# In the attention's tail: two e buffers of three PSUM banks, transposes in the sums' bank, dummies in the projections' bank

## The chip, the core and the metric

The kernel runs on one core of one Trainium2 chip. Its engines work side by side, each in the order of its own program: TensorE (PE) multiplies matrices and transposes, VectorE (DVE) and ScalarE (ACT) work elementwise and read PE's results, GpSimd (POOL) works elementwise on the main on-chip memory, SyncE (SP) issues most of the transfers. PE's results lie in PSUM, which this kernel treats as eight banks of 512 float32 columns for each of 128 partitions. An instruction that needs another engine's result, or a bank that another engine still reads, waits for it, and all that stands behind it on its engine waits too.

The metric is the device time of one execution in microseconds (us), the median of several runs.

## The reference

One transformer block on x of 2048 tokens by 640 features, in float32. The condition c gives six vectors (shift, scale and gate for each half). First half: a layer norm with shift and scale, attention with 32 heads of 20 features in which each token sees itself and the 255 tokens before it, the projection wo, a gate and a residual. Second half: a layer norm with shift and scale, then a channel MLP of width 1536 (which normalises once more), a gate and a residual.

```
scores = jnp.einsum("bhqd,bhkd->bhqk", q, k) * (Dh ** -0.5)
mask = (idx[:, None] - idx[None, :] >= 0) & (idx[:, None] - idx[None, :] < W)
scores = jnp.where(mask[None, None], scores, -1e9)
p = _softmax(scores, axis=-1)
o = jnp.einsum("bhqk,bhkd->bhqd", p, v)
...
x = x + ga * _A_ref(h, A_wqkv, A_wo)
h = _layernorm(x, axis=-1) * (1 + cb) + sb
x = x + gb * _B_ref(h, B_w1, B_b1, B_w2, B_b2)
```

## The kernel before

The attention goes over two halves of the tokens, eight quads of four heads in each, and eight blocks of 128 tokens in each quad: n = 128 items. A loop over t = 0 to 144 (line 1308) runs several stages of this at different lags, and everything that it issues keeps the program's order on each engine.

In iteration t, for t < 128, scores s of item t (queries by keys) are computed for their row maximum (`s_batch`, `s_max`). From LAG = 11 on, scores e of item t - 11 (keys by queries) follow (`e_batch`): four heads with up to 384 columns each. DVE masks e (`e_mask`), ACT takes the exponential into pt (`e_exp`), and POOL cuts two triangles out of pt. At two further iterations' lag the sums o = p v are formed (`pv_stage`, 24 small matmuls) and ACT copies them out to oT (`pv_copy`). The copy stands before `e_exp` in ACT's program, except in the iterations of SUMS_LAST (line 64), where it stands behind it; of 128 to 141 these are 129 to 133, 135, 136 and 139. An item whose mask isn't "do" (the first and the last key block of a quad in the second half: here the items of iterations 130, 131 and 138) has a longer mask and an exponential over 1536 columns instead of 1024.

Besides, a `plan` gives to each quarter h of an iteration other work: the projections before the attention, transposes, and from iteration 115 on the block's next stage for the first token blocks (`mid_steps`): the projection wo (`womm`, tiles in the projections' bank "pp"), the add of its result to x on DVE, layer norms, transposes of x (`xtrans`, tiles xt, copied by ACT to xT) and of y (`ytrans`, tiles yt, read by ACT for yhi and by DVE for ylo). `aside` gives a transpose its bank: "a" before iteration 11, then "o", the bank of the sums, and from iteration 128 on "t", a bank of its own. In iterations 128 to 141 the asides are: 128 the transpose of the row maxima (pm); 129 yt with three blocks; 130 yt with two; 131 xt with four; 132 xt with one; 134 yt; 135 yt; 137 xt with four; 138 xt with one; 140 yt with three; 141 yt with two.

WARM (line 74) puts dummy matmuls into some quarters; before iteration 128 they write the bank "pp", after that a bank of their own, "k". In the tail they stand in 129, 130, 135, 136 and 141.

From iteration 128 on no s is left. That stretch, to the first matmul of the MLP, is the tail; the last e is that of iteration 138, the last sums those of 141. `turn_scores` closes the pools of e and s there and opens e anew.

`width` (line 546) gives the columns between two heads in a score tile: 512 outside of iterations 11 to 127, so that a tile takes four banks and each head has one, and 384 within, so that it takes three and the heads lie across the banks' borders. `cuts` splits a head's product at the borders. The first two of the four slots use one half of the array's rows, the last two the other, and `score_batch` orders the pieces; where both halves write one bank, an empty PE instruction waits for the first half's piece before the second half's is issued.

PSUM in the tail: "pp" one bank from the left, "t" one next to it; "o" the first from the right, then four for e and one for "k". After the loop all pools but the left ones are closed; then `ps_h`, the MLP's first tile, is opened as first pool from the right, and `ps_out` behind it.

```
def aside(shape, name):
    kind = "a" if now[0] < LAG else "o" if now[0] < 2 * NQB * QUADS else "t"
    return pools[kind].tile(shape, F32, tag=kind, name=name)
...
def width():
    return 384 if LAG <= now[0] < 2 * NQB * QUADS else 512
```

Every instruction stands in the profile under line 116, the helper that keeps the order; so the groups are told apart by their tiles (e, s, o, pt, oT, xt, xT, yt, yhi, ylo, wo, warm).

Of the kernel before, what the change touches and what calls it, by code (L numbers as in the profile page):

```python
# [9 lines left out]
F32 = mybir.dt.float32  # L10
# [5 lines left out]
PSUM = bass.MemoryType.PSUM  # L16

P = 128
# [5 lines left out]
NQB = HALF // P  # L24
QUADS = H // 4
# [2 lines left out]
VQ = 4 * VW + 11  # L28
NSLOT = 3
NVB = 5  # L30
LAG = 11
PVLAG = 2
RUN0 = 33
# [40 lines left out]
WARM = {(115, 0): 2, (127, 2): 1, (129, 2): 4, (130, 1): 4, (135, 0): 7, (136, 0): 10, (141, 1): 1}  # L74
# [47 lines left out]
def block_kernel(ctx: ExitStack, tc: tile.TileContext, x, wqkv, wo, w1, b1, w2, b2, c, crow, wmod, wcol, sel, outT):  # L122
# [77 lines left out]
    sco_ctx = ExitStack()  # L200
    pools = {}
# [4 lines left out]
        for name, ctx_, side in (("p", ctx, "left"), ("o", att_ctx, "right"), ("s", sco_ctx, "right"), ("a", sco_ctx, "right")):  # L206
            open_banks(name, ctx_, side)

    def open_banks(name, ctx_, side="right"):
        pools[name] = ctx_.enter_context(  # L210
            tc.tile_pool(name=f"ps_{name}", bufs=1, space=PSUM, side=side, reuse_waits="tile")
        )

    def turn_scores(t, n):

        if t in (LAG, n):
            sco_ctx.close()
            for name in ("e", "s") if t == LAG else ("e",):
                open_banks(name, sco_ctx)

    def aside(shape, name):

        kind = "a" if now[0] < LAG else "o" if now[0] < 2 * NQB * QUADS else "t"
        return pools[kind].tile(shape, F32, tag=kind, name=name)


# [157 lines left out]
    kb_ = [att.tile([P, 2, 256 + HALF], F32R, name=f"kbuf{i}") for i in range(NSLOT)]  # L384
    vq_ = [att.tile([P, NQB, VQ], F32, name=f"vbuf{i}") for i in range(NVB)]
    vcar = att.tile([P, QUADS, 2, VQ], F32, name="vcar")
# [31 lines left out]
    def vblk(half, quad, kb):  # L418
        if half == 1 and kb < 0:
            return vcar[:, quad, kb + 2]  # L420
        return vq_[(half * QUADS + quad) % NVB][:, kb]

# [3 lines left out]
    now = [-1]  # L426
# [12 lines left out]
    def unit(half, kind, j, c2, eng, acc=None, late=False):  # L439
# [44 lines left out]
        def v_turn(b0, nb):  # L484
            def go():
# [13 lines left out]
                for h, d0, n, cnt, r0 in runs:  # L499
                    quad = h // 4  # L500
                    nq = half * QUADS + quad - NVB
                    assert nq < 0 or nq in done_v, (half, j, quad)
                    kb = 4 * c2 + b0
                    dst = vq_[(half * QUADS + quad) % NVB][:, kb : kb + nb]
                    c0 = (h % 4) * VW + d0
# [7 lines left out]
                    if half == 0 and kb + nb == NQB:  # L513

                        last_v[quad] = last_v.get(quad, 0) + cnt * DH + (0 if cnt else n)
                        if last_v[quad] == 4 * DH:
                            nc.gpsimd.tensor_copy(vcar[:, quad], vq_[quad % NVB][:, NQB - 2 : NQB])

# [25 lines left out]
        return t, t.rearrange("p (h n) -> p h n", n=n)[:, :, 0:384]  # L544

    def width():
        return 384 if LAG <= now[0] < 2 * NQB * QUADS else 512

    def cuts(slot, col, n):

# [100 lines left out]
    def e_batch(it):  # L651
        half, quad, i = it["key"]
        t, e = score_banks("e", f"e{half}_{quad}_{i}")
        parts = []
        for h in HEADS:
            pair, r = 2 * quad + h // 2, slice(64 * (h % 2), 64 * (h % 2) + 62)
            parts.append([(
                col, n, kbuf(half, pair)[r, 256 + kb * P : 256 + (kb + 1) * P],
                lambda off, n, q=qbuf(half, pair), r=r, q0=q0: q[r, q0 * P + off : q0 * P + off + n],
            ) for kb, q0, q1, col, n in e_parts(it)[0]])  # L660
        return (t, parts), e

    def e_mask(it, e):
        if it["mask"] == "do":

            nc.vector.copy_predicated(e[:, :, 0:P], masks["d"].to_broadcast([P, 4, P]), e[:, :, 2 * P : 384])
            return
        two = e.rearrange("p h (a n) -> p h a n", n=P)[:, :, 0:3:2]
        nc.vector.copy_predicated(
            two, masks[it["mask"]][:, None].to_broadcast([P, 4, 2, P]), negc[:, None].to_broadcast([P, 4, 2, P])  # L670
        )
# [310 lines left out]
    warm = ps_0.tile([P, P], F32, tag="w0", name="warm")  # L982
# [151 lines left out]
    def take_aside(t, go):  # L1134

        t += AFTER.get(taken[0], 0)
        taken[0] += 1
        while t in asides:
            t += 1
        asides.add(t)  # L1140
        put(t, 1, go)
        return t
# [38 lines left out]
    _, where, turns = lay_units(hi)  # L1181
# [34 lines left out]
    for half in range(2):  # L1216
# [4 lines left out]
        for quad in range(QUADS):  # L1221
            if half or quad:
                js = range(4 * quad * DH // P, (4 * quad * DH + 4 * DH - 1) // P + 1)
                due = 8 * (half * QUADS + quad)
                for c2 in range(2):
                    t = due + 4 * c2 - READ
                    for kind in range(2):
                        t = max([t, due - 8 * NSLOT + LAG + 8] + [over_at.get((kind, j, c2), -9) + 2 for j in js])
                        assert t < due + 4 * c2 - 1, (half, quad, c2, t)
                        put(max(t, 0), 3, lambda half=half, quad=quad, kind=kind, c2=c2: rows_in(half, quad, kind, c2))  # L1230
                        t += 1
    for n, ((g, at), lo) in enumerate(zip(((2, 0), (4, 1), (3, 2)), MODS)):
        steps, rows = mod_steps(g, at)
        spread(plan, [step(1, f) for f in steps], lo[0], lo[1])
        t = int(lo[1])
        for f in rows:
            t = take_aside(t, f) + 1
    for ch, when in turns.items():
# [7 lines left out]
        t = when  # L1246
        for kt in range(KT):
            t = take_aside(t, lambda gos=turn[3 * kt : 3 * kt + 3]: [go() for _, go in gos]) + 1
# [36 lines left out]
    for t, nm, go in sorted(tail, key=lambda e: e[:1]):  # L1285
        t = t if t < 128 else 128 + (t - 128) / LATE
        if nm not in ("load", "om"):
            t = max(t, TOMID)
# [12 lines left out]
    n = len(s_items)  # L1301

    pv_at = {}
    for half in range(2):
        for quad in range(QUADS):
            for qb in range(NQB):
                pv_at.setdefault(LAG + PVLAG + (half * QUADS + quad) * NQB + qb + half, []).append((half, quad, qb))
    for t in range(n + LAG + PVLAG + 4):
        now[0] = t
        si = s_items[t] if t < n else None  # L1310
        u = t - LAG
        ei = e_items[u] if 0 <= u < n else None
        turn_scores(t, n)
        if t == n:
            if WARM:
                pools["k"] = sco_ctx.enter_context(tc.tile_pool(name="ps_k", bufs=1, space=PSUM, side="right"))
            pools["t"] = ctx.enter_context(
                tc.tile_pool(name="ps_t", bufs=1, space=PSUM, side="left", reuse_waits="tile")
            )
        turn_m = 8 <= t <= n and t % 8 == 0  # L1320
        batches = []
        if ei and ei["kbs"]:
            batch, e = e_batch(ei)
            batches.append(batch)
        if si:
            batch, *got = s_batch(si)
            batches.append(batch)
        score_batch(batches)
        if ei and ei["kbs"]:
            e_mask(ei, e)  # L1330
        sums = [(*key, pv_stage(*key)) for key in pv_at.get(t, ())]
        if t not in SUMS_LAST:
            for each in sums:
                pv_copy(*each)
        if ei and ei["kbs"]:
            e_exp(ei, e)
        if t in SUMS_LAST:
            for each in sums:
                pv_copy(*each)
        if si:  # L1340
            s_max(si, *got)
        for h in range(4):
            if (t, h) in WARM:
                ps = pools["k"].tile([P, P], F32, tag="k", name=f"warm{t}_{h}") if t >= n else pools["p"].tile([P, P], F32, tag="pp", name=f"warm{t}_{h}")
                for _ in range(WARM[t, h]):
                    matmul(ps, idn, idn, start=True, stop=True)
            if h == 1:
                rows_out()
            if h == 1 and turn_m:
                m_rows(s_items[t - 1])  # L1350
            for go in plan.pop((t, h), ()):
                go()
        for key in pv_at.get(t, ()):
            pv_store(*key)
    assert not writes and not plan
    sco_ctx.close()
    att_ctx.close()


    mp = ctx.enter_context(tc.tile_pool(name="mp", bufs=1, side="right", reuse_waits="tile"))  # L1360
    ps_h = ctx.enter_context(tc.tile_pool(name="ps_h", bufs=1, space=PSUM, side="right", reuse_waits="tile"))
# [27 lines left out]
    for ch in range(nch):  # L1389
# [24 lines left out]
        for f in range(FT):  # L1414
# [7 lines left out]
            pool, tag = (ps_out, f"o{KT - 1}") if (ch, f) == (0, 1) else (ps_h, "h")  # L1422
# [70 lines left out]
```

## Time and profile before

| what | us |
|---|---|
| median of 3 runs | 977.62 (977.16 to 978.79) |
| the profiled execution, its own time | 978.3 |
| its span, first to last instruction | 976.6 |
| PE busy | 947.7 (97%) |
| DVE busy | 592.9 (61%) |
| POOL busy | 485.8 (50%) |
| ACT busy | 442.4 (45%) |
| weight loads on PE (beside the matmuls) | 752.6 (77%) |
| mean granted clock of TensorE | 0.998 |

A row of the timeline gives the start from the span's start, the duration, the engine, the operation, the tiles as out<-in, their shape, and how many instructions are merged in it; in square brackets stands how long the engine was idle ahead of it and what ended that. The operands in a matmul's name can stand in either order. A PE duration is that of a single pipelined instruction, so the distance between two starts says more. A row of the list of waits gives the waiting engine and tile, what it waited for, and the total, the number and the longest. A row of the table of stretches gives begin and end, length, busy time and number of instructions of PE, PEld (weight loads), DVE, ACT and POOL, the granted clock, and the DMA's share and rate.

### The profile page before, as it was taken

To read this page: it belongs to the slowest core of one execution; us is meant where nothing else is said; L and a number is where in the kernel's file an instruction comes from. 1 tells how busy PE (TensorE), PEld (TensorE's weight loads), DVE (VectorE), ACT (ScalarE), POOL (GpSimd) and SP (SyncE) were. 2 spreads that over 40 slices of the span, in tenths; PEclk is the share of its full clock that TensorE was granted. 3 is DMA by queue.
4 is the path that set the end of the run, shared out by engine and by line. 5 is a ranking of instruction groups with operands and counts; after the bars stand their busy time and mean duration, and the time that the engine had idled before them with its cause. 6 is when DMAs were issued, how large, how long until landed. Compare 5 with 4: busy or idle time off the path is not lost.

```text
span 976.6 us, 20093 instructions
## 1 busy us (share of the span) xinstructions
PE 947.7 (97%) x7789; PEld 752.6 (77%) x7789; DVE 592.9 (61%) x999; ACT 442.4 (45%) x777; POOL 485.8 (50%) x673
## 2 busy tenths in 40 slices
PE   8899999999999999999898999999999999999998
PEld 8677777777777777777677787888888888888886
DVE  6564977978776786767888556563534444342112
ACT  3724555666644545555545654434333243333222
POOL 4423555677864364553646844654554454332121
PEclk9999999999999999999999999999999999999999
DMA  8366778756778459854852245444423342114113
GB/s 307 99 207 199 243 226 260 224 170 168 220 231 236 121 174 283 241 155 120 224 161 76 81 137 161 127 130 138 138 57 103 115 144 85 54 57 145 54 43 119
DMA packets 98974, 152.17 MB, mean 156 GB/s; under 512 B 8864, under 2 KB 42112, under 8 KB 98880
## 3 DMA queue, kind: packets, MB, share of 16 engines
q1 hardware_dynamic: 89664, 142.50, 48.2%
q10 hardware_dynamic: 9216, 8.39, 2.7%
q8 instruction: 62, 1.02, 0.4%
q14 instruction: 32, 0.26, 0.1%
HBM read 98.51 MB, written 51.58 MB: 154 GB/s over the span
## 4 chain that ended last, share of the span: by engine, by line
PE 82%; DVE 7%; ACT 4%; POOL 2%; DMA 2%; issue 2%; SPq 1%; DVEq 0%; POOLq 0%; ACTq 0%
PE pp L116 17%; PE out L116 16%; PE h L116 16%; PE e L116 8%; PE o L116 7%; PE wo L116 7%; PE s L116 4%; ACT pt L116 3%; DVE e L116 2%; PE ppo L116 2%; DVE nm L116 1%; PE yt L116 1%; PE pv L116 1%; PE xt L116 1%; DMA wc<-in_wcol 1%
## 5 line engine op out<-in xcount | busy, mean ns | idle before, releaser
L116 POOL TENSOR_SCALAR_AFFINE_SELECT pt<-pt 128x512 f32<-128x512 f32 x192 | 127.7, 665 | 131.8 <-ACT pt L116 119.4
L116 ACT ACTIVATE pt<-e 128x1024 f32<-128x1024 f32 (+1 forms) x120 | 133.7, 1115 | 67.2 <-DVE e L116 63.8
L116 DVE TENSOR_REDUCE nm<-s 128x1 f32<-128x256 f32 (+5 forms) x212 | 158.0, 779 | 4.4
L116 POOL TENSOR_TENSOR w2lo<-w2r,w2hi 128x640 fp32r<-128x640 f32 x48 | 78.7, 1639 | 160.2 <-ACT w2hi L116 160.2
L116 DVE CAST ghi<-g 128x512 fp32r<-128x512 f32 x48 | 28.1, 585 | 155.7 <-ACT g L116 155.7
L116 PE MATMUL e<-qbuf,kbuf 62*128 62x128 f32 (+2 forms) x773 | 112.8, 330 | 9.1 <-ACT pt L116 7.6
L116 PEld LDWEIGHTS e<-qbuf,kbuf 62*128 62x128 f32 x773 | 81.2, 186 | 48.5 <-ACT pt L116 23.2
L116 PE MATMUL pp<-hhi,w_hi 128*128 128x512 f32 x265 | 113.4, 428 | 0.2 <-ACT pf L116 0.2
L116 PE MATMUL s<-kbuf,qbuf 60*128 60x384 f32 (+2 forms) x728 | 106.6, 303 | 4.0 <-DVE nm L116 1.6
L116 PE MATMUL pp<-hlo,w_hi 128*128 128x512 f32 x265 | 108.1, 408 | 1.3 <-POOL hlo L116 1.3
L116 DVE COPY_PREDICATED e<-mask_t,e 128x512 f32<-128x512 uint32 x96 | 66.6, 694 | 66.2 <-PE e L116 62.6
L116 PE MATMUL pp<-hhi,w_lo 128*128 128x512 f32 x265 | 106.8, 403 | 0.0
L116 PEld LDWEIGHTS s<-kbuf,qbuf 60*128 60x128 f32 x728 | 89.8, 187 | 14.0 <-DVE nm L116 6.1
L116 PE MATMUL o<-pt,vbuf 128*32 128x128 f32 x2688 | 99.6, 277 | 0.7 <-ACT xT L116 0.7
L116 PE MATMUL out<-ghi,w2hi 128*128 128x512 f32 x240 | 95.5, 398 | 0.5 <-ACT g L116 0.5
L116 PE MATMUL out<-glo,w2hi 128*128 128x512 f32 x240 | 94.0, 391 | 0.0
L116 PE MATMUL out<-ghi,w2lo 128*128 128x512 f32 x240 | 93.9, 391 | 0.0
L116 POOL TENSOR_TENSOR w_lo<-wraw,w_hi 128x128 fp32r<-128x128 f32 x171 | 76.0, 475 | 32.6 <-ACT w_hi L116 32.6
L116 PE MATMUL h<-yhi,w1hi 128*128 128x512 f32 x220 | 87.8, 399 | 0.0
L116 PE MATMUL h<-ylo,w1hi 128*128 128x512 f32 x220 | 86.2, 392 | 0.0
L116 PE MATMUL h<-yhi,w1lo 128*128 128x512 f32 x220 | 86.0, 391 | 0.0
L116 DVE COPY_PREDICATED s<-mask_t,s 128x512 f32<-128x512 uint32 x112 | 77.1, 689 | 11.8 <-PE s L116 11.5
(179 smaller groups left out, 1839.0 us busy)
## 6 DMA issues: line engine op xcount, KB each, us to landing
w2r<-in_w SPq DMA_DIRECT2D x48, 320.0 KB
qbuf<-q_scr SPq DMA_DIRECT2D x60, 240.0 KB
wraw<-in_wqkv SPq DMA_DIRECT2D x36, 320.0 KB
kbuf<-k_scr SPq DMA_DIRECT2D x44, 240.0 KB
q_scr<-stage SPq DMA_DIRECT2D x20, 512.0 KB
k_scr<-stage SPq DMA_DIRECT2D x20, 512.0 KB
o_scr<-oT ACTq DMA_DIRECT2D x64, 128.0 KB
wm<-in_wmod SPq DMA_DIRECT2D x20, 320.0 KB
```

The lines of the kernel that those rows point to most:

```text
L116: return self.tc.keep_in_program_order(op(*args, **kw))
```

## The change

From iteration 128 on e has a pool of two buffers, and the distance between heads stays 384, so that a buffer takes three banks: six in all, beside "pp" and "o". The banks "t" and "k" are not there: transposes use the sums' bank "o" to the end of the loop, and dummies the bank "pp". After the loop "t" is opened for the MLP.

```diff
+END = 1000
...
-    def open_banks(name, ctx_, side="right"):
+    def open_banks(name, ctx_, side="right", bufs=1):
         pools[name] = ctx_.enter_context(
-            tc.tile_pool(name=f"ps_{name}", bufs=1, space=PSUM, side=side, reuse_waits="tile")
+            tc.tile_pool(name=f"ps_{name}", bufs=bufs, space=PSUM, side=side, reuse_waits="tile")
         )
...
             for name in ("e", "s") if t == LAG else ("e",):
-                open_banks(name, sco_ctx)
+                open_banks(name, sco_ctx, bufs=1 if t == LAG else 2)
...
-        kind = "a" if now[0] < LAG else "o" if now[0] < 2 * NQB * QUADS else "t"
+        kind = "a" if now[0] < LAG else "o" if now[0] < END else "t"
...
     def width():
-        return 384 if LAG <= now[0] < 2 * NQB * QUADS else 512
+        return 384 if LAG <= now[0] else 512
...
         turn_scores(t, n)
-        if t == n:
-            if WARM:
-                pools["k"] = sco_ctx.enter_context(tc.tile_pool(name="ps_k", bufs=1, space=PSUM, side="right"))
-            pools["t"] = ctx.enter_context(
-                tc.tile_pool(name="ps_t", bufs=1, space=PSUM, side="left", reuse_waits="tile")
-            )
...
-                ps = pools["k"].tile([P, P], F32, tag="k", name=f"warm{t}_{h}") if t >= n else pools["p"].tile([P, P], F32, tag="pp", name=f"warm{t}_{h}")
+                ps = pools["p"].tile([P, P], F32, tag="pp", name=f"warm{t}_{h}")
...
     att_ctx.close()
-
+    now[0] = END
+    pools["t"] = ctx.enter_context(tc.tile_pool(name="ps_t", bufs=1, space=PSUM, side="left", reuse_waits="tile"))
```

## The prediction

> **What bounds the kernel now.** I read first where the span goes, then the stretch that the change touches, then its waits.
>
> ```profile
> span 976.6 us, 20093 instructions
> 538.08:578.07 39.99, 38.46 (x537) 30.64 (x537) 22.33 (x46) 24.56 (x43) 27.10 (x43) 1.00 0.27 80
> PEld e L116 <- ACT pt L116: 3.0, 6, 1.1
> PE e L116 <- ACT pt L116: 1.3, 2, 0.9
> ```
>
> The second line is the table of stretches (length, then busy time of PE, PEld, DVE, ACT, POOL, then clock) for the attention's tail, from the first scores of iteration 128 to the first matmul of the MLP. TensorE (PE) is busy 38.46 of 39.99 us there, at full clock, so the tail ends when PE has got through its program. PE executes in program order: each wait of one of its instructions delays everything behind it, and each microsecond added to the tail is added to the end, since what follows is matmuls again. The last two lines are the list of waits in the tail (total, times, longest): the scores e wait for the exponential (ACT, pt) of the tile before. That is what a second buffer can take away: 1.3 us as gaps between matmuls, at most 3.0 us as gaps between weight loads. I take 2.4, since some 0.1 us of each of the six load gaps is the normal step from one group to the next (an estimate).
>
> **The change part by part.** The tail's own order on PE, with every edited place in it:
>
> ```profile
> 538.08 0.62 PE L116 MATMUL e<-qbuf,kbuf 62*128 62x384 f32 x4
> 538.63 0.86 PE L116 MATMUL o<-pt,vbuf 128*32 128x128 f32 x24
> 539.42 0.28 PE L116 MATMUL pm<-idn,nm 128*32 128x128 f32 x1
> ...
> 541.01 0.62 PE L116 MATMUL e<-qbuf,kbuf 62*128 62x384 f32 x4 [0.42 <-ACT pt L116]
> ...
> 542.36 0.55 PE L116 MATMUL yt<-idn,y 128*128 128x128 f32 x3
> ...
> 543.73 0.68 PE L116 MATMUL e<-qbuf,kbuf 62*128 62x256 f32 x8
> ...
> 546.12 0.38 PE L116 MATMUL yt<-idn,y 128*128 128x128 f32 x2
> 547.36 0.73 PE L116 MATMUL e<-qbuf,kbuf 62*128 62x128 f32 x8 [0.86 <-ACT pt L116]
> ...
> 549.36 0.60 PE L116 MATMUL xt<-idn,xb 128*128 128x128 f32 x4
> ...
> 550.97 0.62 PE L116 MATMUL e<-qbuf,kbuf 62*128 62x384 f32 x4
> ...
> 552.86 0.27 PE L116 MATMUL xt<-idn,xb 128*128 128x128 f32 x1
> ...
> 556.37 0.62 PE L116 MATMUL e<-qbuf,kbuf 62*128 62x384 f32 x4
> ...
> 557.72 0.55 PE L116 MATMUL yt<-idn,y 128*128 128x128 f32 x3
> ```
>
> These are iterations 128 to 132 and 134. In each the transpose (pm, yt, xt) comes 1.34, 1.35, 2.39, 2.00, 1.89 and 1.35 us after its e. It writes a bank of its own, so it does not ask whether the sums o of the same iteration have been copied out.
>
> First, **e in three banks**. At 384 columns a head the four heads' products fall on bank borders: six pieces instead of four (nine instead of eight where a tile has two key blocks), and the middle bank is written by both halves of the array, so a wait for the first half's piece stands before the last. The trace has the same six pieces in the same order, alone, as scores s in the main loop:
>
> ```profile
> 153.62 0.89 PE L116 MATMUL s<-kbuf,qbuf 60*128 60x256 f32 x6
> 154.44 0.75 PE L116 MATMUL o<-pt,vbuf 128*32 128x128 f32 x20
> ```
>
> From the first piece to the next group 0.82 us pass; for four pieces (538.08 to 538.63) 0.55. So +0.27 us for each of eleven e tiles, 3.0 us. Below it could be 0 if the wait cost nothing; above, 0.54 a tile if the nine-piece tiles stop twice. I take 0.27, from the row of the same shape.
>
> Second, **transposes in the sums' bank**. A transpose must now wait for the copy oT of that iteration's sums, and the next sums for the copy of the transpose. The main loop, which already does this, shows both waits:
>
> ```profile
> 509.69 0.28 PE L116 MATMUL pm<-idn,nm 128*32 128x128 f32 x1 [1.11 <-ACT oT L116]
> 516.12 0.86 PE L116 MATMUL o<-pt,vbuf 128*32 128x128 f32 x24 [0.74 <-ACT xT L116]
> ```
>
> How long it takes is a chain through DVE and ACT, of which these are the steps:
>
> ```profile
> 539.56 0.27 ACT L116 COPY oT<-o 128x128 f32<-128x128 f32 x1 [1.54 <-PE o L116]
> 541.74 0.70 DVE L116 COPY_PREDICATED e<-mask_t,e 128x512 f32<-128x512 uint32 x1 [0.62 <-PE e L116]
> 542.48 1.02 ACT L116 ACTIVATE pt<-e 128x1024 f32<-128x1024 f32 x1 [0.21 <-DVE e L116]
> 543.39 0.26 ACT L116 COPY oT<-o 128x128 f32<-128x128 f32 x1
> ...
> 548.14 1.29 DVE L116 COPY_PREDICATED_SCALAR e<-mask_t,negc 128x1024 f32 x1
> 549.47 1.46 ACT L116 ACTIVATE pt<-e 128x1536 f32<-128x1536 f32 x1 [0.28 <-DVE e L116]
> 550.82 0.26 ACT L116 COPY oT<-o 128x128 f32<-128x128 f32 x1
> ```
>
> ACT runs in program order too. Where the iteration is not in SUMS_LAST the copy comes before the exponential: it starts 0.93 after o (538.63 to 539.56), takes 0.27, and ACT's end reaches PE 0.04 later (549.47 + 1.46 to 550.97); with e's 0.82 before it, the transpose can start 2.06 after e. Where the iteration is in SUMS_LAST the copy stands behind the exponential, and that behind the mask, and that behind e: 0.73 (541.01 to 541.74) + 0.27, then 0.74 to the exponential, 0.91 to the copy, 0.27 and 0.04, in all 2.96 after e. With the long mask and exponential of the tiles that have no causal pair: 0.78 + 0.27 + 1.33 + 1.35 + 0.26 + 0.04 = 4.03. By this:
>
> - 128 (not last): from 1.34 to 2.06, +0.72. Here pm is the maximum's transpose.
> - 129 (last): from 1.35 to 2.96, +1.61.
> - 130 and 131 (last, long): from 2.39 and 2.00 to 4.03, +1.64 and +2.03.
> - 132 (last): from 1.89 to 2.96, +1.07.
> - 134 (not last): from 1.35 to 2.06, +0.71.
> - 133, 135, 136 and 137: no new wait; in 133 there is no transpose, in 135 the seven dummies stand ahead of it, in 136 there is none, in 137 nine matmuls stand ahead. Only e's pieces, 4 x 0.27 = +1.08.
>
> Those are +8.86, e's pieces counted in. The tail's end has three more places:
>
> ```profile
> 569.66 0.53 PEld L116 LDWEIGHTS e<-qbuf,kbuf 62*128 62x128 f32 x8 [0.35 <-ACT pt L116]
> 572.25 0.86 PE L116 MATMUL o<-pt,vbuf 128*32 128x128 f32 x24
> ...
> 575.90 0.55 PE L116 MATMUL yt<-idn,y 128*128 128x128 f32 x3
> 576.82 0.86 PE L116 MATMUL o<-pt,vbuf 128*32 128x128 f32 x24
> 577.00 0.56 DVE L116 TENSOR_TENSOR ylo<-yt,yhi 128x384 fp32r<-128x384 f32 x1 [2.94 <-ACT yhi L116]
> 577.93 0.38 PE L116 MATMUL yt<-idn,y 128*128 128x128 f32 x2
> 578.07 0.49 PE L116 MATMUL h<-yhi,w_hi 128*128 128x512 f32 x1
> 578.76 0.42 DVE L116 TENSOR_TENSOR ylo<-yt,yhi 128x256 fp32r<-128x256 f32 x1 [0.81 <-ACT yhi L116]
> ```
>
> - 138: the transpose x1 is copied out behind the long exponential, 1.05 + 1.33 + 1.35 + 0.26 + 0.04 = 4.03 after e, and the sums of 139 now wait for it. Before they came 2.59 after e (569.66 to 572.25): +1.44.
> - 140: the sums of 141 wait until ylo has read yt: 575.90 to 577.56 is 1.66, and 0.04; before they came 0.92 after yt: +0.78.
> - 141: yt waits for the sums' copy, 0.93 + 0.27 + 0.04 = 1.24 after o. And the MLP's first tile h is laid in the bank that o leaves (both are the first pool opened from the right), so it waits for the last ylo: 578.76 + 0.42 - 577.93 = 1.25, and 0.04. So h comes 2.53 after o, before 1.25 (576.82 to 578.07): +1.28.
>
> Third, **dummies in the projections' bank**: they now wait for the add that reads it. In 129, 130, 135 and 136 the transposes or e keep PE later than that add anyhow; in 141 the wait for the copy covers it. Cost 0; uncovered it would be under the 0.49 of one add each (an estimate from ylo's rows of like size). Nothing moves past SP's or POOL's queues; what they carry in the tail shifts with it.
>
> The sum: 8.86 + 1.44 + 0.78 + 1.28 = 12.4, less the e waits, 2.4: +10.0 us. Note that in every iteration above the transpose starts after the copy that follows the exponential, or PE has work until then: the second buffer is hardly ever used ahead of time, and the wait for e has turned into a longer one for o. Behind the tail a little may come back, since PE waits once for ACT there and DMAs would be relatively earlier:
>
> ```profile
> 588.40 0.50 PE L116 MATMUL out<-ghi,w2hi 128*128 128x512 f32 x1 [0.52 <-ACT g L116]
> ```
>
> Between 0 and 0.52; I take 0.4. So +9.6. The profiled execution took 978.3 us (span 976.6), 0.7 over the median 977.62 of the runs shown; on the median that is 987.2.
>
> **The rivals.** A clock drop. In the main loop one gap was followed by a slower PE clock:
>
> ```profile
> 488.51 0.55 PE L116 MATMUL e<-qbuf,kbuf 62*128 62x128 f32 x5 [2.00 <-ACT pt L116]
> 490.00:492.00 2.00, 2.00 (x29) 1.78 (x20) 1.97 (x3) 1.26 (x2) 0.00 (x0) 0.60 0.00 0
> ```
>
> The gap was 2.00 us, and the granted clock (third column from the end) 0.60 in the next stretch: 0.8 us lost in 2 us. The tail now has no such gap and clock 1.00. The new waits come near it: in 131 the transpose starts 4.03 after e, of which e, o and one step of the projection fill about 2.2, so some 1.8 us are empty, with 1.3 to 1.4 empty in 129 and 130 just before (estimates from the rows above). One drop costs 0.8 to 1.6 us; at 1.2 the time is 988.4. The Trainium skill (TensorE: Matmul & The Clock Gate, Why this matters for your kernels) asks only that gaps between bursts of matmuls stay under about 3 us. By that rule no drop follows and 987.2 stands; the row above shows a drop after a gap of 2.00 us, so the trace does not agree, and I keep the drop as a case.
>
> The pieces of e cost nothing: if the wait in front of the last piece is covered, 11 x 0.27 = 3.0 fall away: 984.2. For it speaks that in the main loop two tiles' pieces are woven into each other; against it that in the tail e stands alone, as s does in the quoted row.
>
> The waits for e stay beside those for o, so that the second buffer does nothing at all: 987.2 + 2.4 = 989.6. Against it: by the walk above PE reaches the next e later than the exponential ends, so there is nothing left to wait for.
>
> The other side: the sums' copy is never late. The place is ACT's order in 129 to 132, the price the transposes' waits; if these and the pieces' cost vanish, the e waits are all that is left: 977.6 - 2.4 = 975.2. It decides at the copy's end against PE's arrival: in 129 PE has finished o 1.6 us after e, the copy ends 2.9 after it, so it would have to end 1.3 us sooner. For it speaks that ACT is busy only 24.56 of 39.99 us; against it that the copy's place behind the exponential is program order, and that the exponential's own start hangs on the mask. The Trainium skill (Perfetto Trace Analysis, Optimization Strategy) says that one gap recurring on the engine that should be full can mean too few buffers for the next tile. By that rule alone the recurring waits for e go and the time is this rival's; the trace agrees that the gaps recur (six of them) but not that they are large.
>
> **How the numbers follow.** The forecast, +9.6 to 987.2, has 0.52; a clock drop (988.4) 0.27; free pieces (984.2) 0.12; e waits that stay (989.6) 0.04; the other side 0.05, of which I give 0.03 to faster and 0.02 to a result where only half of it holds. Faster or slower means by over 0.2%, about 2 us, which is what a measurement of this kernel can tell from no change. All cases but the last lie above that: slower 0.95, same 0.02, faster 0.03. The range: down by free pieces (3.0) and e waits at their upper end (0.6) to 983.6; up by e waits at 1.3 instead of 2.4 (1.1), nothing given back behind the tail (0.4), the pieces' upper end (three times 0.27, 0.8) and one drop (1.2) to 990.7. The cases left out hold under 2 in 10.
>
> **What would show it right or wrong.** In the profile of the changed kernel the tail, from the first e without s to the first h, should last about 50 us instead of 40. PE's waits there should name ACT oT ahead of pm, yt and xt (1.3 to 1.9 us each in 129 to 131), ACT xT ahead of the sums of 139 (over 1 us) and DVE ylo ahead of the sums of 141 and of h; waits of e for ACT pt should be near 0. From the first piece of an e tile to o about 0.82 us. A granted clock under 1.00 in the tail would show the drop. I am wrong if transposes start within 0.2 us of the matmul ahead of them in 129 to 132, or if the tail is under 45 us.

## The result and the profile after

| | before | changed |
|---|---|---|
| median of four runs each, us | 977.39 (976.78 to 978.79) | 986.71 (986.50 to 989.09) |
| the profiled execution, us | 978.3 | 986.5 |
| its span, us | 976.6 | 984.8 |
| mean granted clock | 0.998 | 0.998 |

The changed kernel is slower: the ratio of the times is 1.0091, with a 95% interval from 1.0078 to 1.0104. On the medians it loses 9.3 us, between the two profiled executions 8.2.

The table of stretches of the changed kernel, for its tail and for all that follows it (length, busy time of PE, PEld, DVE, ACT and POOL, granted clock, DMA):

```profile
537.64:588.13 50.49, 42.42 (x557) 33.67 (x556) 23.24 (x48) 25.60 (x45) 26.68 (x43) 1.00 0.26 78
588.13:984.80 396.67, 392.52 (x1900) 330.37 (x1900) 165.26 (x297) 133.04 (x211) 167.18 (x170) 1.00 0.35 106
```

The stretch behind the tail in the kernel before, from the same view:

```profile
578.07:976.60 398.53, 393.10 (x1903) 330.32 (x1901) 166.07 (x298) 133.74 (x212) 167.44 (x170) 1.00 0.35 108
```

So the 8.2 us split into three: the tail went from 39.99 to 50.49 (+10.50), what follows it from 398.53 to 396.67 (-1.86), and what precedes it from 538.08 to 537.64 (-0.44, in code that the change doesn't touch: in the profile of before the clock falls to half there for 3.41 us from 490 on, in that of the changed kernel it doesn't, and the groups ahead of 490 differ by 0.02 us only). PE is busy only 42.42 of 50.49 us in the tail, where it was busy 38.46 of 39.99: it now waits. The list of PE's waits in the changed kernel's tail (total, times, longest) names for what:

```profile
PE yt L117 <- ACT oT L117: 2.8, 3, 1.3
PE xt L117 <- ACT oT L117: 2.0, 2, 1.4
PE o L117 <- ACT xT L117: 1.0, 1, 1.0
PE h L117 <- DVE ylo L117: 0.9, 1, 0.9
PE o L117 <- DVE ylo L117: 0.7, 1, 0.7
PE pm L117 <- ACT oT L117: 0.4, 1, 0.4
```

The waits of e for pt are gone from this list, and 7.8 us of waits that were not there before have come: of transposes for the sums' copy (oT), of sums for what reads a transpose (xT, ylo), and of h for the last ylo. PE's timeline shows them in place:

```profile
537.64 0.89 PE L117 MATMUL e<-qbuf,kbuf 62*128 62x256 f32 x6
538.45 0.86 PE L117 MATMUL o<-pt,vbuf 128*32 128x128 f32 x24
539.70 0.28 PE L117 MATMUL pm<-idn,nm 128*32 128x128 f32 x1 [0.39 <-ACT oT L117]
...
540.80 0.89 PE L117 MATMUL e<-qbuf,kbuf 62*128 62x256 f32 x6
...
543.75 0.55 PE L117 MATMUL yt<-idn,y 128*128 128x128 f32 x3 [1.28 <-ACT oT L117]
...
545.12 0.94 PE L117 MATMUL e<-qbuf,kbuf 62*128 62x128 f32 x9
...
549.08 0.44 PE L117 MATMUL yt<-idn,y 128*128 128x128 f32 x2 [1.14 <-ACT oT L117]
549.45 0.88 PE L117 MATMUL e<-qbuf,kbuf 62*128 62x256 f32 x9
...
553.34 0.66 PE L117 MATMUL xt<-idn,xb 128*128 128x128 f32 x4 [1.40 <-ACT oT L117]
554.80 0.89 PE L117 MATMUL e<-qbuf,kbuf 62*128 62x256 f32 x6
...
557.69 0.33 PE L117 MATMUL xt<-idn,xb 128*128 128x128 f32 x1 [0.57 <-ACT oT L117]
...
580.23 0.86 PE L117 MATMUL o<-pt,vbuf 128*32 128x128 f32 x24 [1.04 <-ACT xT L117]
...
585.52 0.86 PE L117 MATMUL o<-pt,vbuf 128*32 128x128 f32 x24 [0.72 <-DVE ylo L117]
...
588.13 0.50 PE L117 MATMUL h<-yhi,w_hi 128*128 128x512 f32 x1 [0.92 <-DVE ylo L117]
```

Two distances are to be read here. From e to o it is 0.81 now (537.64 to 538.45), with six pieces in e. (With nine it is 0.87 in 130 and 138. It is 0.99 in 131 and also in 136, which has six pieces: there the sums also wait a little for the ylo that reads the transpose of the iteration before, as the run with transposes in o alone shows, 1.00 and 0.99 with four banks for e.) From e to the transpose it is 2.06 in iteration 128 (537.64 to 539.70), 2.95 in 129, 3.96 in 130, 3.89 in 131 and 2.89 in 132. And the second buffer is not used ahead: ACT's timeline for iteration 129 shows why.

```profile
542.52 1.02 ACT L117 ACTIVATE pt<-e 128x1024 f32<-128x1024 f32 x1 [0.65 <-DVE e L117]
543.44 0.26 ACT L117 COPY oT<-o 128x128 f32<-128x128 f32 x1
```

The exponential that frees the first buffer ends at 543.54, the next e starts at 545.12, since the transpose between them waits for the copy that stands behind that very exponential.

### The profile page after: what moved, and what is told of

The parts are those of the page before. It is cut to its first block, busy times and chain, and to the rows that moved or that the text cites. A ratio compares the mean times of both kernels' runs of the same rounds, so it can differ in the third digit from the quotient of the medians.

```text
span 984.8 us, 20136 instructions
## 1 busy us (share of the span) xinstructions
PE 951.1 (97%) x7808; PEld 756.1 (77%) x7808; DVE 593.0 (60%) x999; ACT 442.5 (45%) x777; POOL 485.6 (49%) x673
## 4 chain that ended last, share of the span: by engine, by line
PE 86%; DVE 5%; ACT 4%; issue 3%; POOL 1%; DVEq 0%; ACTq 0%; POOLq 0%
PE pp L117 18%; PE h L117 17%; PE out L117 16%; PE e L117 8%; PE o L117 8%; PE wo L117 7%; PE s L117 5%; ACT pt L117 3%; DVE e L117 2%; PE ppo L117 2%; PE warm L117 1%; PE yt L117 1%; DVE nm L117 1%; PE xt L117 1%; PE pv L117 1%
## 5 line engine op out<-in xcount | busy, mean ns | idle before, releaser
L117 PE MATMUL e<-qbuf,kbuf 62*128 62x128 f32 (+2 forms) x792 | 115.1, 326 | 8.4 <-ACT pt L117 7.2
L117 PEld LDWEIGHTS e<-qbuf,kbuf 62*128 62x128 f32 x792 | 83.9, 185 | 48.1 <-ACT pt L117 20.8
L117 ACT COPY oT<-o 128x128 f32<-128x128 f32 x128 | 33.8, 264 | 114.5 <-PE o L117 109.4
```

Of the source, the lines that this page charges most:

```text
L117: return self.tc.keep_in_program_order(op(*args, **kw))
```

## The experiments

The theory: the tail is longer because transposes and sums share a bank, while the sums' copy stands behind the exponential in ACT's order; three banks for e add the pieces; the second buffer brings next to nothing; behind the tail some of it comes back because the weights' transfers are then earlier relative to h. Against it stand the other readings that the prediction names (a clock drop, free pieces, the buffer) and one more: that the dummies' new bank is to blame. All tails below run from the first e of iteration 128 to the first h, as above.

| kernel | median us (range) | ratio to before, 95% | tail us |
|---|---|---|---|
| three banks alone | 981.05 (980.34 to 983.26) | 1.0027 (1.0016 to 1.0038) | 42.23 |
| transposes in o alone | 986.94 (985.17 to 988.98) | 1.0093 (1.0076 to 1.0109) | 48.29 |
| dummies in pp alone | 979.98 (978.23 to 980.86) | 1.0014 (1.0005 to 1.0023) | 40.39 |
| changed, one buffer | 989.94 (987.75 to 990.72) | 1.0113 (1.0098 to 1.0128) | 52.22 |
| changed, run again | 988.07 (986.64 to 989.05) | 1.0105 (1.0088 to 1.0122) | 50.78 |
| changed, one buffer, again | 988.61 (987.58 to 990.18) | 1.0112 (1.0097 to 1.0127) | 52.22 |
| changed, sums first | 983.28 (982.81 to 985.30) | 1.0060 (1.0045 to 1.0075) | 46.49 |
| sums first, one buffer | 983.95 (983.55 to 985.16) | 1.0065 (1.0050 to 1.0080) | 46.94 |
| changed, h elsewhere | 988.68 (988.22 to 989.64) | 1.0117 (1.0103 to 1.0130) | 50.91 |
| sums first, fewer dummies | 983.87 (982.20 to 984.38) | 1.0063 (1.0048 to 1.0079) | 45.61 |
| before, fewer dummies | 978.47 (977.64 to 980.41) | 1.0012 (1.0004 to 1.0021) | 39.81 |
| before, w1 first | 977.33 (976.54 to 978.52) | 0.9992 (0.9983 to 1.0001) | 39.99 |

The kernel before had medians of 978.35, 977.80, 977.57 and 978.54 beside the four groups of runs (the first four rows, the next four, the next three, the last).

### Three banks alone

```diff
 def width():
-        return 384 if LAG <= now[0] < 2 * NQB * QUADS else 512
+        return 384 if LAG <= now[0] else 512
```

> The kernel before with one part of the change: in the tail e lies in three banks (384 columns a head), still one buffer; transposes and dummies keep banks of their own. Theory A (the sums' bank costs most; the pieces cost 0.27 us for each of eleven e tiles): tail 40.0 + 3.0 = 43.0 us, 980.4 us. Rival B (the pieces are what costs, through the wait between the halves of the array): tail near the 50.5 us of the changed kernel, 985 us or more. If the pieces were free: 977.4.

The tail in this kernel's table of stretches:

```profile
540.17:582.40 42.23, 41.13 (x556) 33.67 (x555) 22.74 (x47) 24.37 (x43) 26.87 (x43) 1.00 0.26 74
```

What is left of e's waits in the list of waits:

```profile
PE e L116 <- ACT pt L116: 1.0, 2, 0.8
```

The tail grew by 2.24 us with PE's busy time up 2.67. The pieces do cost time, about what eleven tiles by 0.27 give (2.97), but a part of it fell into waits for pt that were there anyhow: iterations 128, 130 and 137, which ended in such a wait of the matmuls or of their weight loads, grew by only 0.06, 0.17 and 0.09. The median is 981.05, where 980.4 was expected. This ends the case of free pieces.

### Transposes in o alone

```diff
-        kind = "a" if now[0] < LAG else "o" if now[0] < 2 * NQB * QUADS else "t"
+        kind = "a" if now[0] < LAG else "o" if now[0] < 1000 else "t"
...
     att_ctx.close()
-
+    now[0] = 1000
```

> The kernel before with one part of the change: in the tail transposes use the sums' bank; e keeps four banks and one buffer, dummies their own bank. Theory A: the changed kernel's added waits without the pieces, 9.4 us, less the e waits that they cover, 2.4: tail 47 us; some 1.8 come back behind the tail as in the changed kernel, so 982.6 us. Rival B: nearly no change, tail 40 to 41 us, 977.4 to 978.4. Rival C (the dummies' bank): no change.

Here e has one buffer of four banks, as before. The stretches of the tail and behind it:

```profile
538.51:586.80 48.29, 39.75 (x538) 30.67 (x537) 22.94 (x48) 25.70 (x45) 27.06 (x43) 1.00 0.28 82
586.80:983.50 396.70, 392.52 (x1900) 330.40 (x1900) 165.39 (x297) 132.80 (x211) 166.81 (x170) 1.00 0.35 106
```

And the list of PE's waits in this kernel's tail:

```profile
PE yt L116 <- ACT oT L116: 2.8, 3, 1.3
PE xt L116 <- ACT oT L116: 2.0, 2, 1.3
PE o L116 <- DVE ylo L116: 1.4, 3, 0.7
PE o L116 <- ACT xT L116: 1.0, 1, 1.0
PE h L116 <- DVE ylo L116: 0.9, 1, 0.9
PE pm L116 <- ACT oT L116: 0.4, 1, 0.4
```

This one edit gives +8.30 of the +10.50 and nearly the changed kernel's list of waits. With the pieces' +2.24 it makes 10.54, against 10.50 in the changed kernel. More tells the second part of the finding: there is no wait of e for pt in this list, though e has a single buffer. The shared bank removes those waits by itself, because PE now arrives later. Behind the tail 396.70, 1.83 under the 398.53 before: the give-back comes with this edit too. Both numbers missed their expectation: the tail is 1.3 us longer than the 47 expected, and the median of 986.94 is 4.3 over 982.6. The kernel before was itself about 1 us slower in this group than the 977.4 that was reckoned with, the profiled execution took 985.17 with a mean clock of 0.998, and the other three, with 0.990 to 0.994, took 986.51 to 988.98; where their clock fell isn't on record.

### Dummies in pp alone

```diff
-            if WARM:
-                pools["k"] = sco_ctx.enter_context(tc.tile_pool(name="ps_k", bufs=1, space=PSUM, side="right"))
...
-                ps = pools["k"].tile([P, P], F32, tag="k", name=f"warm{t}_{h}") if t >= n else pools["p"].tile([P, P], F32, tag="pp", name=f"warm{t}_{h}")
+                ps = pools["p"].tile([P, P], F32, tag="pp", name=f"warm{t}_{h}")
```

> The kernel before with one part of the change: in the tail dummies write the projections' bank. Theory A: nothing in 129 to 136; in 141 the dummy waits about 0.3 to 0.4 us for the add ahead of it, 977.4 to 977.8 us, tail 40.0 to 40.4. Rival C (dummies wait for adds that come late): 979 us or more.

The tail was 40.39 (+0.40), all of it in iteration 141, where the dummy waits for the add; the list of waits has it:

```profile
PE warm L116 <- DVE xb L116: 0.3, 1, 0.3
```

The four other places cost nothing. The median is 1.6 over that of before; 1.2 of it is not in the tail of the profiled execution. It goes with the clock: the five of the ten executions with a mean clock of 0.994 or less average 980.64 us, the other five 978.95, and of the sixteen of the kernel before only one is as low as 0.994. Where the clock fell in them, and whether the dummies' bank has to do with it, stays open.

### One buffer, and the changed kernel once more

```diff
-                open_banks(name, sco_ctx, bufs=1 if t == LAG else 2)
+                open_banks(name, sco_ctx, bufs=1)
```

> The changed kernel with one e buffer of three banks in the tail instead of two. Theory A (in every iteration the transposes or other work keep PE past the end of the exponential, so the second buffer is never used ahead): as the changed kernel, tail 50.5 us within 0.4, 986.7 us. Rival D (the second buffer does save the 2.4 us of e waits, and the rest costs the more): tail 52.9, 989.1 us.

The tail came out 1.73 us longer than in the changed kernel, at 52.22, and the median of 989.94 is nearer to rival D's 989.1 than to theory A's 986.7. But no wait of e for pt was in the tail, which is what rival D needs. So both kernels ran once more, on one chip.

> The changed kernel once more, as the neighbour of the next three. Tail 50.5 us where no clock drop falls into it, and 986 to 988 us; with a drop of the clock in the tail, as the run with one buffer had, 1.5 us more.

> The changed kernel with one e buffer, timed beside the changed kernel. Theory A (the second buffer is never used ahead; the first run's extra 1.7 us in the tail were a clock drop that depends on where the clock's window falls): every iteration without a drop as long as in the changed kernel, within 0.05 us, medians within 1.5 us of each other. Rival D (the second buffer saves e waits): PE's e waits for ACT pt in the tail, 2 us or more slower with two overlapping nowhere.

In these executions the granted clock (third column from the end of the table of stretches) was under 1.00 in a part of the tail. In the changed kernel run again, in iteration 131:

```profile
551.40:554.80 3.40, 3.04 (x31) 2.25 (x24) 1.03 (x1) 1.74 (x3) 3.03 (x4) 0.51 0.00 0
```

With one buffer again, in 131 and 132 (the first run with one buffer is alike):

```profile
551.40:557.92 6.52, 5.46 (x49) 4.39 (x48) 1.69 (x2) 3.39 (x5) 3.41 (x4) 0.63 0.07 23
```

The clock fell to half there, for 6.83 us with one buffer (both times), for 3.41 us in the changed kernel run again. Iteration 131 took 6.54 and 6.54 us with one buffer and 5.64 with two, against 5.35 in the changed kernel's first profile; 132 took 4.05 and 4.04 with one buffer, against 3.59. That makes 1.65 of the 1.73 us by which the one-buffer tail was longer, and the whole 0.29 of the second profile of the changed kernel. The other iterations agree within 0.02, but for 138 with one buffer (0.08 longer). So where the clock stayed up, the second buffer was worth nothing that these profiles show. The medians of the second group differ by 0.54 us with overlapping ranges. Yet over both groups the four shortest of eight executions with two buffers took 986.50 to 986.77 us, and the shortest of eight with one took 987.58. So a gain of about 1 us by another way than the waits of e is not ruled out; whether one buffer makes the drop more frequent can't be told from so few profiles.

### Sums first, with two buffers and with one

The copy of the sums goes ahead of the exponential in the eight iterations of the tail that had it last.

```diff
-SUMS_LAST = [14, 15, 18, 25, 27, 29, 35, 42, 43, 59, 63, 64, 69, 74, 76, 79, 83, 86, 87, 88, 90, 91, 92, 95, 101, 103, 105, 106, 110, 111, 113, 117, 120, 121, 122, 123, 126, 129, 130, 131, 132, 133, 135, 136, 139]
+SUMS_LAST = [14, 15, 18, 25, 27, 29, 35, 42, 43, 59, 63, 64, 69, 74, 76, 79, 83, 86, 87, 88, 90, 91, 92, 95, 101, 103, 105, 106, 110, 111, 113, 117, 120, 121, 122, 123, 126]
```

> The changed kernel with the tail's iterations taken out of SUMS_LAST, so that the sums' copy stands ahead of the exponential there. Theory A: transposes start 2.06 us after e in 129 (from 2.96), about 2.65 in 130 (from 3.95), 2.4 in 131 (from 3.89), 2.2 in 132 (from 2.89); tail 50.5 - 4.4 = 46 us, 982.3 us. Rival B (pieces): no change, 986.7. If the copy weren't what the transposes wait for: no change either.

> The same with one e buffer. Here PE reaches the next e before the exponential ends in one place, after 130, by about 0.9 us. Theory A: tail 0.9 us longer than with two buffers, 983.2 us. So the second buffer is worth something only once the copy is out of the way. If it is worth the whole 2.4 us of e waits: 984.7; if nothing: 982.3.

The tail with two buffers:

```profile
538.91:585.40 46.49, 41.78 (x557) 33.72 (x556) 23.09 (x48) 25.55 (x45) 26.73 (x43) 1.00 0.29 86
```

A new wait in it, of the sums of iteration 131 (PE's timeline):

```profile
549.98 0.86 PE L117 MATMUL o<-pt,vbuf 128*32 128x128 f32 x24 [0.68 <-DVE ylo L117]
```

With one buffer, a wait of e in the list of waits:

```profile
PE e L117 <- ACT pt L117: 0.8, 1, 0.8
```

With two buffers the tail fell from 50.49 to 46.49, as expected, with only the place of the copy changed: ACT's order makes 4.0 of the 10.5 us. The transposes of 129 to 132 now start 2.06, 2.66, 2.89 and 2.15 us after e, instead of 2.95, 3.96, 3.89 and 2.89. Only the one in 131 is off (2.4 expected), by the wait of its sums for ylo shown above. PE is early enough now for the second buffer to matter, and in the tail it is worth 0.45 us (46.94 - 46.49), half of what I expected; the medians, 983.28 and 983.95, have overlapping ranges and don't show it. With one buffer iteration 130 is 0.84 longer (3.80 against 2.96), by the wait for pt, and 132 by 0.19; but 131 is 0.56 shorter (3.74 against 4.30), since with two buffers PE comes to the sums of 131 sooner and waits there for ylo, the 0.68 above. (The profiled execution with two buffers is the slowest of its four, 985.30: its clock was at 0.50 for 3.41 us right behind the tail, and the stretch behind the tail took 398.20 instead of 396.60 with one buffer.)

Still 46.49 is 6.5 over before. Of this 3.5 lies in 138, 140 and 141 (4.04, 2.99 and 2.61, before 2.59, 2.27 and 1.25), which the place of the copy in 129 to 136 doesn't reach, and the pieces alone gave 2.2.

### h in another bank

```diff
-    ps_h = ctx.enter_context(tc.tile_pool(name="ps_h", bufs=1, space=PSUM, side="right", reuse_waits="tile"))
     ps_out = ctx.enter_context(tc.tile_pool(name="ps_out", bufs=1, space=PSUM, side="right", reuse_waits="tile"))
+    ps_h = ctx.enter_context(tc.tile_pool(name="ps_h", bufs=1, space=PSUM, side="right", reuse_waits="tile"))
```

> The changed kernel with the MLP's output pool opened ahead of the pool of h, so that h does not lie in the bank that o leaves. Theory A: h starts right behind the last transposes, about 1.2 us earlier, tail 49.3 us. Theory E (what came back behind the tail came back because h waited while the transfers behind the tail went on): that part grows by as much, from 396.7 to about 397.9 us, and the time stays 986.5 to 988 us. If both were independent: 985.3 to 986.5.

Both stretches of this kernel:

```profile
538.79:589.70 50.91, 44.86 (x557) 35.86 (x556) 22.74 (x46) 24.77 (x43) 26.63 (x43) 0.93 0.25 73
589.70:987.30 397.60, 392.74 (x1902) 330.37 (x1900) 165.97 (x298) 133.77 (x212) 167.11 (x170) 1.00 0.35 107
```

And the only wait of PE behind its tail:

```profile
PE wo L117 <- POOL ot_lo L117: 0.7, 1, 0.7
```

Iteration 141 got shorter by 1.16 us, as expected (in the tail's sum a clock drop of 6.83 us in 131 and 132 hides it). But behind the tail 0.93 of it was lost again: a wait of `wo` for POOL, which the changed kernel doesn't have, came back. The net gain is 0.2 us in the two stretches without the drop; on the medians there is none (988.68, over the 988 that was expected at most).

### Where the give-back comes from

The kernel before has two waits of PE behind the tail (list of waits):

```profile
PE wo L116 <- POOL ot_lo L116: 0.7, 1, 0.7
PE out L116 <- ACT g L116: 0.5, 1, 0.5
```

The changed kernel has neither. What differs is the order of h and of the transfer of the MLP's weights w1r, on SP's queue, before:

```profile
574.16 3.98 SPq L116 DMA_DIRECT2D wm<-in_wmod  x5
578.24 3.22 SPq L116 DMA_DIRECT2D w1r<-in_w  x2
```

and in the changed kernel:

```profile
580.67 6.18 SPq L117 DMA_DIRECT2D wm<-in_wmod  x5
586.95 3.14 SPq L117 DMA_DIRECT2D w1r<-in_w  x2
```

Before, w1r was issued 0.17 us after h (578.24 against 578.07); in the changed kernel 1.18 ahead of it (586.95 against 588.13), for h now waits longer than the queue does. ACT's timeline of the kernel before shows how a late transfer gets to PE: ACT waits for the weights w2r, the next transfer behind w1r on SP's queue, and g stands behind that in ACT's order.

```profile
587.04 0.73 ACT L116 CAST w2hi<-w2r 128x640 fp32r<-128x640 f32 x1 [1.69 <-DMA w2r<-in_w]
```

If the lateness of these transfers is the cause, the kernel before gains the same when w1r is issued ahead of wm:

```diff
+    w1_load(2)
     wm5 = [mp.tile([P, D], F32, name=f"wm5_{kt}") for kt in range(KT)]
...
-        if ch == 0:
-            w1_load(2)
```

> The kernel before with one transfer moved, no part of the change: the MLP's third weight tile w1r is issued ahead of the five wm transfers instead of behind them, since the wait that vanished behind the changed kernel's tail was for data asked for there. If w1r behind wm on SP's queue is what makes PE wait 0.52 us (out for g) and 0.72 us (wo for ot_lo) behind the tail: the first or both go, the part behind the tail shrinks from 398.5 to 397.3 to 398.0 us, 976.4 to 977.1 us, faster than both kernels. If those waits hang on w2r or r instead, which stay where they are: no change, 977.6 us.

The first issue of w1r in this kernel (SP's queue), ahead of wm now:

```profile
573.97 0.47 SPq L116 DMA_DIRECT2D w1r<-in_w  x1
```

And the stretch behind its tail:

```profile
577.91:974.80 396.89, 392.75 (x1902) 330.66 (x1900) 167.22 (x298) 133.65 (x212) 167.02 (x170) 1.00 0.35 108
```

PE has no wait at all behind this tail, and the stretch is 396.89 instead of 398.53, 1.64 less; the changed kernel had 1.86 less. So how early these transfers are issued relative to h accounts for most of the give-back. Which of them PE waits for this run doesn't separate, since w2r came earlier together with w1r: 3.24 us after h, much as in the changed kernel (3.47), and not 5.97 as before. It speaks for w2r that w1r was issued 0.17 after h in three of the kernels here, before, with fewer dummies and with three banks alone, while the wait of `out` for g was 0.5, 0.9 and 1.2, in the order in which w2r came 5.97, 6.22 and 6.47 after h. As a kernel it has the lowest median of all (977.33 against 978.54 beside it), but the interval of its ratio just includes 1: a gain is likely and not shown.

### Fewer dummies, two misses

The 17 dummies of iterations 135 and 136 are left out; nothing reads what they compute.

```diff
-WARM = {(115, 0): 2, (127, 2): 1, (129, 2): 4, (130, 1): 4, (135, 0): 7, (136, 0): 10, (141, 1): 1}
+WARM = {(115, 0): 2, (127, 2): 1, (129, 2): 4, (130, 1): 4, (141, 1): 1}
```

First in the kernel with the sums first:

> The run with the sums' copy first and two buffers, without the 17 dummies of iterations 135 and 136, which compute nothing that is used. 135 becomes 1.2 us shorter (the transpose then waits for the copy), 136 2.4 us; w00 in 137 may wait up to 1 us for POOL's ot_lo. Tail 46.5 - 2.6 to 3.6 = 43 to 44 us, 979.5 to 981 us; 1 to 2 us more if the clock drops there. Still slower than before, since the pieces and the waits for o at 138, 140 and 141 remain.

Then in the kernel before:

> The kernel before without the 17 dummies of iterations 135 and 136. There PE would then wait for the exponential instead: 0.3 us shorter in 135 and 1.1 us in 136, tail 38.6 us, 976.4 us with the clock kept; 977.5 to 979 us if the dummies are what keeps the clock up there.

With the sums first the tail came to 45.61 instead of the expected 43 to 44 (from 46.49), in the kernel before to 39.81 instead of 38.6 (from 39.99); neither median fell: with the sums first it is 983.87 (983.28 with the dummies, in another group), and in the kernel before 978.47 beside 977.57, slower by a little with the whole interval above 1. Iterations 135 and 136 did get shorter, with the sums first from 3.58 and 4.22 to 2.43 and 2.07, but 137 grew from 3.56 to 5.62. ACT's timeline there, with the sums first:

```profile
569.54 0.92 ACT L117 ACTIVATE y<-xb,nra,rsa 128x640 f32<-128x640 f32 x1 [2.57 <-POOL nra L117]
```

And PE's:

```profile
570.66 0.66 PE L117 MATMUL xt<-idn,xb 128*128 128x128 f32 x4 [1.83 <-ACT oT L117]
```

The dummies had covered a chain through POOL: ACT stands 2.57 us for `nra`, and everything behind it in its order stands too, the copy oT with it. In the profiles the dummies cost next to nothing, because PE would have waited in their place. With the sums first and fewer dummies the clock was at 0.50 for 3.41 us behind the first h, and the stretch behind the tail took 398.30 instead of about 396.6, the 1 to 2 us that were expected for a drop. In the profile of the kernel before, the clock in the tail stayed 1.00 without the dummies. That they don't keep the clock up is not shown by this one execution: the median lies in the range that was expected if they do (977.5 to 979), and three of its eleven executions, like three of fifteen of the kernel before, have a mean clock of 0.993 or less.

## Why the prediction was right, and where its terms were off

The forecast of +9.6 met +9.3 on the medians, and +10.3 where the changed kernel ran again (988.07 beside 977.80). Step by step:

- **Transposes behind the sums' copy.** Forecast 2.06, 2.96, 4.03, 4.03, 2.96 and 2.06 us after e in 128 to 132 and 134; measured 2.06, 2.95, 3.96, 3.89, 2.89 and 2.06. The walk along ACT's program order was right, and the run with the sums first shows that this order is the cause of 4.0 us. The gaps ahead of the transposes in 129 to 131 (1.28, 1.14, 1.40) are at or under the low end of the 1.3 to 1.9 that were given as a sign.
- **The tail's end.** Iteration 138 grew by 1.37 (forecast 1.44), 140 by 0.72 (0.78), 141 by 1.36 (1.28).
- **Pieces of e.** The length from e to o is 0.81 with six pieces (forecast 0.82). That they cost time of their own is shown by the run with three banks alone; that it is 2.24 there and not 3.0 is the cover of the waits for pt.
- **The waits of e that go.** Taken at 2.4 us. All terms of the tail without this sum to 12.4, and the tail grew by 10.50, so 1.9 is what is left for it. (The 0.1 taken off each of the six gaps was an estimate that no run tests by itself.) It shows mostly in 128 (+0.23 instead of +0.72) and 130 (+0.70 instead of +1.64), each of which ended in a wait of e, by 0.42 and 0.86, in the rows of before; 131 and 137 are 0.29 and 0.19 under their forecast. In 136 the prediction saw no new wait, and it grew by 0.44 instead of 0.27, since its sums wait for ylo. The second buffer has no part in this, by the run with transposes in o alone.
- **Dummies in pp.** Forecast 0. Alone they cost 0.40 in 141, under the 0.49 that was given as the bound; in the changed kernel the wait for the copy covers it there, as forecast: 141 grew by 1.36 against a forecast of 1.28 without them.
- **Behind the tail.** The mis-sized term: 0.4 with 0.52 as its upper end, measured 1.86. I had looked at one wait in that stretch; there are two, and the second, 0.72 us of `wo` for POOL, was not in the bound. By the starts of the instructions right behind the two that waited, 0.8 of the give-back falls up to the first and another 1.05 between them: h comes 10.06 us later than before, the first of them 9.27, the second 8.22.

The sum of tail and give-back came out 1.0 us lower than forecast in the profiled execution (+8.64 against +9.6), and what precedes the tail took another 0.44, by the clock drop at 490 that only the profile of before has. That the medians are nearer to it (+9.3) is in part because the profiled execution of before is itself 0.9 over its median; that the number fits so well is luck, as the +10.3 of the second group says.

Of the rivals, the **clock drop** is real but not in every execution: none in the tail of the changed kernel's first profile, 0.29 us in that of the second, 1.65 with one buffer (forecast 1.2). The slowest run of the first group (989.09) had the lowest mean clock, 0.993 against 0.997 and 0.998 in the others, so the drop may make the upper end of the range; where it lay in that run isn't on record. **Free pieces** are ruled out by the three banks alone, **waits of e that stay** by the list of waits. The **other side** needed a sums' copy that is never late; it was late in six iterations, and even with the sums first the tail is longer than before.

## What to carry to other kernels

Before a buffer is doubled with banks that something else gives up, follow the order on PE and ask which wait ends last ahead of the instruction that is to run early. Here a transpose had to share a bank with sums whose copy is queued behind the exponential, so PE reached the next scores after the one buffer was free already. And when a wait is lengthened, look at what else was tied with it: a late h made a weight transfer early, which gave back a fifth of what the tail lost, and most of that came without any loss, in the profile, by moving that transfer alone (1.64 of 1.86 us; on the medians the gain is likely and not shown).

## What the runs showed of the hardware

The granted clock fell to half for 3.41 or for 6.83 us (twice that) in iterations 131 and 132 of four executions: the changed kernel's second profile, both with one buffer, and the one with h elsewhere. In the changed kernel's first profile and in those of transposes in o alone and of the sums first, with two buffers and with one, the tail kept 1.00. With the sums first and two buffers it fell right behind the tail. The same program thus had the drop and did not have it; what decides is open. The gap of 2.00 us in the main loop is another such case. The clock of before falls behind it, as the prediction shows; the changed kernel's first profile has the same gap and no drop:

```profile
488.49 0.55 PE L117 MATMUL e<-qbuf,kbuf 62*128 62x128 f32 x5 [2.01 <-ACT pt L117]
490.00:492.00 2.00, 1.61 (x28) 1.18 (x20) 1.97 (x3) 1.28 (x2) 0.00 (x0) 1.00 0.00 0
```

In the clock records of all fourteen traces every stretch between two changes of the clock is a whole number of 3.41 us (10.24, 58.03 and 471.04 us are 3, 17 and 138 times that). This fits a clock that is set anew every 3.41 us, so that an execution has the drop or not by where these points fall among its gaps; no run here tests that. In the tail the drop began in 131, behind gaps that were 1.28 and 1.14 us long in the changed kernel's rows above, in 129 and 130. The Trainium skill (TensorE: Matmul & The Clock Gate, Why this matters for your kernels) asks for gaps under about 3 us; these executions don't agree with that as a bound, and neither does the drop behind the gap of 2.00 us in the main loop of before.

A drop of 3.41 us cost only 0.29. The changed kernel's second profile shows why, in PE's timeline for iteration 131:

```profile
550.23 0.88 PE L117 MATMUL e<-qbuf,kbuf 62*128 62x256 f32 x9
...
554.12 0.94 PE L117 MATMUL xt<-idn,xb 128*128 128x128 f32 x4 [0.36 <-ACT oT L117]
```

The transpose still starts 3.89 after e, and its wait is 0.36 instead of 1.40: the slower matmuls filled the gap that the shared bank had made. A long wait hides a part of the clock drop that stands beside it.
